# Small matmul tiles for the first two batches' packing attention, and the converted w_out kept in its raw tile

## The chip, the cores and the metric

One core of a Trainium2 chip runs the whole kernel. The metric is the device time of one execution in microseconds (us). A profile is one further execution, taken by the hardware profiler; its span runs from the first to the last recorded instruction.

## The reference

Eight batches of eight heads attend twice: 32 learned "pack" queries p attend to the 576 keys and values of a head, and then the 576 queries q attend to the 32 packed results. Two mixture layers follow on the 4608 x 512 result. The weights of all layers arrive as float32 in the listing below and as float64 words in the kernel.

```python
def sm_attn(qq, kk, vv):
    s = scale * np.matmul(qq, kk.transpose(0, 1, 3, 2))
    s = s - np.max(s, axis=-1, keepdims=True)
    a = np.exp(s)
    a = a / (np.sum(a, axis=-1, keepdims=True) + 1e-09)
    return np.matmul(a, vv)
p_packed = sm_attn(p, k, v)            # pp: 32 x 64 for each head
x = sm_attn(q, p_packed, p_packed)     # 576 x 64 for each head
# x is reshaped to (4608, 512)
h = x @ w_in                           # 512 -> 2048
g = np.maximum(h, 0.0) + alpha * np.minimum(h, 0.0)
x = g @ w_out                          # 2048 -> 512
g = x @ w_gate                         # 512 -> 1536
silu = g * (1.0 / (1.0 + np.exp(-g)))
return silu * (x @ w_val) @ w_out2     # 1536 -> 512
```

## The kernel before

**Folding.** The result of the second attention is never formed. Since it is a2 · pp, with a2 the second softmax, the kernel multiplies pp by w_in once for each batch (ppw, `L811`) and then computes h = a2 · ppw (`L316` to `L318`, three matmuls of high and low parts for one product: a2l x high, a2h x high, a2h x low). g (`L1060`) is split into hi (`L1068`, ScalarE) and lo (`L1070`, GpSimd), and acc = g · w_out is again three matmuls (`L1083`, `L1084`, `L1089`).

**Groups.** A batch has two groups of four heads. The first two batches (groups 0 and 1, then 2 and 3) go through the functions shown at the end of this section, step by step: kT by transposes (`L390`), scores s10 and s11 of p against the two halves of the keys (`logits`, `L417`), their maximum (`L430`, VectorE), E = exp (`L438`, ScalarE), transposes of E, pp (`s_pp`, `L481`), its transpose ppT (`s_ppt`), scores s20 and s21 of q against pp (`logits` again, with the queries read with a stride), the second softmax on VectorE (`L513` to `L550`) and its split into a2h (`L551`) and a2l (`L552`). Later batches use other functions, of which two rows serve below as prices: `L580`, scores by head on 64 x 32 tiles of the array into two banks of PSUM, and `L710`, pp by head on 96 x 32 tiles.

**Weights.** w_in and w_out are fetched by 16 loads (`fetch`, one DMA queue, in order) into raw tiles of float64 words. `widen` makes float32 of them in the raw tile and a second tile `val`: an absolute value on ScalarE (`L234`), five VectorE steps (`L236` to `L267`; `L263` and `L265` replace the last one for four pieces), and a sum on GpSimd (`L277`) that leaves the number in `val`. For w_in, `val` is the weight's own tile; for w_out it is a scratch (`cvd`, and after its two halves are used always `cvb`). `round_piece` then scales it by the signs of alpha (`L301`), rounds it to the high part (`L304`, both ScalarE), and subtracts for the low part (`L305`, GpSimd). The pieces come in a fixed order, here called i0, i2, ... for w_in and o0, o2, ... for w_out: i2 i0 o0 i4 i6 o2 o4 o6 i10 i8 i14 i12 o8 o10 o12 o14. The raw tiles are cva0, cva1, cvc0 and cvc1.

**Order.** The order in which each engine takes its instructions is worked out when the kernel is built: the code issues work word by word from a script ("c" converts a piece, "r" rounds one, "1" does both), and a list scheduler with a timing model of its own reorders it on all engines, for about the first 37 steps of h and acc (the first 215 us). From there on the order of TensorE is written out. Instructions on one engine run in that order and wait there.

Of the kernel before, what the change touches and what calls it, by code (L numbers as in the profile page):

```python
# [11 lines left out]
AF = mybir.ActivationFunctionType  # L12
ALU = mybir.AluOpType
# [4 lines left out]
P = 128  # L18
# [46 lines left out]
BY_POOL = {0, 2, 5, 11}  # L65
# [36 lines left out]
def f32(ap):  # L102
    return ap.bitcast(F32)
# [3 lines left out]
def tile_kernel(  # L107
# [23 lines left out]
    nc = tc.nc  # L131
    B, H, S, D = q.shape
# [6 lines left out]
    HQ = 4  # L139
    M6 = 6  # L140
    PB = S // M6
    NB32 = S // 32
    HS = S // 2
# [57 lines left out]
    def like(ap, other):  # L201

        if len(other.shape) == 2:
            return ap
        return ap.rearrange("p (c f) -> p c f", c=other.shape[1])

    raws, vals, borrowed, queue, marks, spots = [], [], [], [], {}, {}
    fetched, loaded, unsplit = [], [], []
    begun, made, rounded = {}, {}, {}

    def halves_of(ap):

        n = ap.shape[1]
        if len(ap.shape) == 2 and n == 512:
            return [ap]
        return [ap[:, i * n // 2 : (i + 1) * n // 2] for i in range(2)]

    def load():

        src, parts, f = queue.pop(0)  # L220
        raw = raws.pop(0)
        fetch(like(raw, src), src)
        loaded.append((raw, parts, f))
# [3 lines left out]
        with tc.issue_after(fetched[-1].ins) if fetched else ExitStack():  # L227
            fetched.append(nc.sync.dma_start(out=out, in_=in_))

    def widen(raw, val, by_pool=False):  # L230

        words = raw.rearrange("p (n t) -> p n t", t=2)
        low, high = (like(words[:, :, i], val) for i in range(2))
        nc.scalar.activation(out=f32(val), in_=f32(high), func=AF.Abs)  # L234
        yield "v"
        nc.vector.tensor_scalar(  # L236
            out=f32(val), in0=f32(val), scalar1=E_TOP, scalar2=E_LOW, op0=ALU.min, op1=ALU.max
        )
        yield "v"
        nc.vector.tensor_scalar(  # L240
            out=val,
            in0=val,
            scalar1=3,
            scalar2=0x3FFFFFF8,
            op0=ALU.logical_shift_left,
            op1=ALU.bitwise_and,
        )
        yield "v"
        nc.vector.scalar_tensor_tensor(
            out=val,  # L250
            in0=high,
            scalar=0xC0000000,
            in1=val,
            op0=ALU.bitwise_and,
            op1=ALU.bitwise_or,
        )
        yield "v"
        nc.vector.tensor_scalar(
            out=high, in0=val, scalar1=0xFF800000, scalar2=None, op0=ALU.bitwise_and
        )  # L260
        yield "v"
        if by_pool:
            nc.scalar.activation(out=f32(low), in_=low, func=AF.Copy, scale=2.0**-52)  # L263
            for a, b in zip(halves_of(f32(low)), halves_of(f32(high))):
                nc.gpsimd.tensor_tensor(out=a, in0=a, in1=b, op=ALU.mult)  # L265
        else:
            nc.vector.scalar_tensor_tensor(  # L267
                out=f32(low),
                in0=low,
                scalar=2.0**-52,  # L270
                in1=f32(high),
                op0=ALU.mult,
                op1=ALU.mult,
            )
        yield "p"
        for a, b in zip(halves_of(f32(val)), halves_of(f32(low))):
            nc.gpsimd.tensor_tensor(out=a, in0=a, in1=b, op=ALU.add)  # L277

    def convert():

        raw, parts, f = loaded.pop(0)
        dst = parts()
        spots["piece"] = spots.get("piece", -1) + 1
        if f is None:
            val = dst[0].bitcast(U32)
        else:
            val = vals.pop(0) if len(vals) > 1 else vals[0]
        for _ in widen(raw, val, spots["piece"] in BY_POOL):
            pass
        if queue and (spots["piece"] < 4 or not any(raw is t for t in borrowed)):  # L290
            raws.append(raw)
            load()
        unsplit.append((dst, val, f))

    def round_piece():

        dst, val, f = unsplit.pop(0)
        for i in range(2 if f is not None else 0):
            hi, lo = (t[:, i, :] for t in dst)
            full = like(f32(val), dst[0])[:, i, :]  # L300
            nc.scalar.activation(  # L301
                out=full, in_=full, func=AF.Copy, scale=sg[:, f + i : f + i + 1]
            )
            nc.scalar.activation(out=hi, in_=full, func=AF.Copy)  # L304
            nc.gpsimd.tensor_tensor(out=lo, in0=full, in1=f32(hi), op=ALU.subtract)  # L305

    def scratch(name):
        return wpool.tile([P, 2048], U32, tag="D", name=name, bufs=WBUFS["D"])
# [4 lines left out]
    def mm3(o, wts, xs, start, stop, **kw):  # L313
        whi, wlo = wts
        xhi, xlo = xs
        nc.tensor.matmul(o, wlo, xhi, start=start, stop=False, **kw)  # L316
        nc.tensor.matmul(o, whi, xhi, start=False, stop=False, **kw)  # L317
        return nc.tensor.matmul(o, whi, xlo, start=False, stop=stop, **kw)  # L318

    ident = sm.tile([P, P], F32, name="ident")  # L320
    make_identity(nc, ident)
# [9 lines left out]
    def quad(g, ptags=("at",), evac=nc.scalar):  # L331
# [78 lines left out]
        def logits(lhs, rhs, half, name, turned=False):  # L410
            t = pst([P, 512], f"{name}{half}")
            for pr in range(2):
                x = rhs[pr][:, half * HS : (half + 1) * HS]
                if turned:
                    x = rhs[pr].rearrange("q (m p) -> q p m", m=M6)
                    x = x[:, half * PB // 2 : (half + 1) * PB // 2, :]
                nc.tensor.matmul(  # L417
                    t[64 * pr : 64 * pr + 64, :HS],
                    lhs[:, 64 * pr : 64 * pr + 64],
                    x,  # L420
                    start=True,
                    stop=True,
                )
            return t

        def s_s1():
# [48 lines left out]
        def s_pp():  # L475
            pp = pst([P, 512], "pp")
            for m in range(M6):
                for pr in range(2):
                    e = st["ET"][m // 4]
                    c = (m % 4) * P + 64 * pr  # L480
                    nc.tensor.matmul(  # L481
                        pp[64 * pr : 64 * pr + 64, :P].rearrange("p (h d) -> p h d", h=2),
                        e[:PB, c : c + 64],
                        st["v"][:, 2 * pr : 2 * pr + 2, m, :],
                        start=(m == 0),
                        stop=(m == M6 - 1),
                    )
            pb = ppbd[g % 2]
            for h in range(HQ):
                r = slice(32 * h, 32 * h + 32)  # L490
                c = slice((h % 2) * D, (h % 2) * D + D)
                marks[f"pp{g}"] = nc.scalar.activation(
                    out=pb[r, c], in_=pp[r, c], func=AF.Copy, scale=st["rs"][r, 3:4]
                )

        def s_ppt():
# [292 lines left out]
    def pp_win(b, j):  # L789

        t = wtile("C", F32R, f"ppw{b}_{j}")
        ppw[b, j] = t
        (w,) = win[j]
        if b > 1:
            o = [
                ps.tile([P, 512], F32, tag="at", name=f"ppw{b}_{j}{r}", bufs=2) for r in range(2)
            ]
            heads8(o, ppT[b, None], [w[:, i, :] for i in range(H // 2)])
            for r in range(2):
                nc.scalar.activation(out=t[:, r, :], in_=o[r], func=AF.Copy)  # L800
            for r in range(2):
                nc.vector.tensor_tensor(
                    out=t[:, NQ + r, :], in0=o[r], in1=f32(t[:, r, :]), op=ALU.subtract
                )
            return
        for q2 in range(NQ):
            o = ps.tile([P, 512], F32, tag="at", name=f"ppw{b}_{j}{q2}", bufs=2)
            with behind():
                for pr in range(2):
                    r = slice(64 * pr, 64 * pr + 64)  # L810
                    last = nc.tensor.matmul(  # L811
                        o[r, :], ppT[b, q2][:, r], w[:, 2 * q2 + pr, :], start=True, stop=True
                    )
            done(last)
            nc.scalar.activation(out=t[:, q2, :], in_=o, func=AF.Copy)
            nc.vector.tensor_tensor(
                out=t[:, NQ + q2, :], in0=o, in1=f32(t[:, q2, :]), op=ALU.subtract
            )
# [27 lines left out]
    def run(script):  # L846
        for word in script.split():
            word, _, held = word.partition(":")
            with ExitStack() as behind_marks:
                for name in held.split(",") if held else ():  # L850
                    behind_marks.enter_context(tc.issue_after(marks[name].ins))
                for w in ("c", "r") if word == "1" else (word,):
                    do(w)

    def do(word):
        if word in early:
# [558 lines left out]
```

## Time and profile before

| what | us |
|---|---|
| three runs | 1646.09, 1644.81, 1646.09 (median 1646.09) |
| the profiled execution | 1643.74 |
| its span | 1642.0 |
| TensorE busy in it | 1591.0 (97%) |
| VectorE, ScalarE, GpSimd busy | 848.1, 678.0, 717.1 |

The profiled execution took 1.7 us more than its span and 2.35 us less than the median of the runs. TensorE is idle for about 50 us of the span in all.

### The profile page before, as it was taken

To read this page: it belongs to the slowest core of one execution; us is meant where nothing else is said; L and a number is where in the kernel's file an instruction comes from. 1 tells how busy PE (TensorE), PEld (TensorE's weight loads), DVE (VectorE), ACT (ScalarE), POOL (GpSimd) and SP (SyncE) were. 2 spreads that over 40 slices of the span, in tenths; PEclk is the share of its full clock that TensorE was granted. 3 is DMA by queue.
4 is the path that set the end of the run, shared out by engine and by line. 5 is a ranking of instruction groups with operands and counts; after the bars stand their busy time and mean duration, and the time that the engine had idled before them with its cause. 6 is when DMAs were issued, how large, how long until landed. Compare 5 with 4: busy or idle time off the path is not lost.

```text
span 1642.0 us, 28420 instructions
## 1 busy us (share of the span) xinstructions
PE 1591.0 (97%) x10709; PEld 1446.6 (88%) x10709; DVE 848.1 (52%) x1473; ACT 678.0 (41%) x1504; POOL 717.1 (44%) x764
## 2 busy tenths in 40 slices
PE   7599999999999999999999999999999999999997
PEld 4368899989899999999999999999999999999996
DVE  6858757676767676765224433432442443334222
ACT  6575655555555655555312322322232232223212
POOL 4738665666666666664223223222322232322222
PEclk8699999999999999999999999999999999999999
DMA  9405365655545564653644564554465465435442
GB/s 286 147 28 136 111 181 143 158 139 157 153 132 154 137 166 117 171 158 106 243 155 173 180 218 138 196 200 171 158 215 183 150 214 177 180 139 214 149 165 84
DMA packets 224058, 266.11 MB, mean 162 GB/s; under 512 B 128160, under 2 KB 185520, under 8 KB 223920
## 3 DMA queue, kind: packets, MB, share of 16 engines
q1 hardware_dynamic: 223920, 264.30, 50.8%
q8 instruction: 84, 1.38, 0.3%
q14 instruction: 54, 0.44, 0.1%
HBM read 214.70 MB, written 49.55 MB: 161 GB/s over the span
## 4 chain that ended last, share of the span: by engine, by line
issue 38%; PE 37%; POOL 16%; DVE 5%; ACT 2%; DMA 1%; POOLq 0%; ACTq 0%; DVEq 0%
POOL pl L1302 9%; PE acc L1083 7%; PE acc L1084 7%; PE acc L1089 7%; POOL s L1282 4%; PE h L316 4%; PE h L318 4%; PE h L317 3%; PE ppw L580 1%; PE s L580 1%; POOL cva L277 1%; PE s L417 1%; POOL lo L1070 1%; POOL xr L1143 0%; PE pp L710 0%
## 5 line engine op out<-in xcount | busy, mean ns | idle before, releaser
L1070 POOL TENSOR_TENSOR lo<-g,hi 128x288 fp32r<-128x288 f32 x256 | 233.4, 913 | 236.1 <-ACT hi L1068 188.9
L1282 POOL TENSOR_TENSOR s<-s,u 128x384 f32<-128x384 f32 x72 | 73.0, 1015 | 490.1 <-ACT s L1276 490.1
L1060 DVE SCALAR_TENSOR_TENSOR g<-h,sg,m 128x288 f32<-128x288 f32 x256 | 130.5, 511 | 173.5 <-ACT m L1057 142.4
L1239 DVE TENSOR_TENSOR u<-yb,p 128x384 f32<-128x384 f32 x144 | 80.1, 556 | 254.8 <-PE yb L318 254.8
L1302 POOL TENSOR_TENSOR pl<-s,ph 128x384 fp32r<-128x384 f32 x144 | 145.4, 1031 | 106.8 <-ACT ph L1300 106.8
L1239 DVE TENSOR_TENSOR u<-vb,u 128x384 f32<-128x384 f32 x144 | 80.4, 558 | 197.6 <-PE vb L318 197.4
L316 PE MATMUL h<-a2h,ppw 128*128 128x288 f32 x512 | 159.4, 311 | 16.0 <-ACT a2h L551 9.1
L318 PE MATMUL o<-wp,ph 128*128 128x512 f32 x432 | 171.5, 397 | 0.0
L317 PE MATMUL o<-wp,ph 128*128 128x512 f32 x432 | 170.9, 396 | 0.0
L316 PE MATMUL o<-wp,pl 128*128 128x512 f32 x432 | 168.7, 391 | 0.9 <-POOL pl L1302 0.9
L1057 ACT ACTIVATE m<-h,sal 128x288 f32<-128x288 f32 x256 | 126.9, 497 | 101.4 <-PE h L318 100.9
L1276 ACT ACTIVATE s<-p 128x384 f32<-128x384 f32 x72 | 37.9, 526 | 301.7 <-DVE p L1239 301.7
L1068 ACT ACTIVATE hi<-g 128x288 fp32r<-128x288 f32 x256 | 113.0, 442 | 111.4 <-DVE g L1060 108.7
L318 PE MATMUL h<-a2l,ppw 128*128 128x288 f32 x512 | 152.2, 298 | 2.2 <-POOL a2l L552 2.2
L317 PE MATMUL h<-a2h,ppw 128*128 128x288 f32 x512 | 152.1, 297 | 0.0
L316 PE MATMUL yb<-ring,gv 128*128 128x384 f32 x432 | 145.9, 338 | 0.3 <-DVE u L1239 0.3
L317 PE MATMUL yb<-ring,gv 128*128 128x384 f32 x432 | 144.4, 334 | 0.0
L318 PE MATMUL yb<-ring,gv 128*128 128x384 f32 x432 | 144.4, 334 | 0.0
L316 PEld LDWEIGHTS h<-a2h,ppw 128*128 128x128 f32 x512 | 97.5, 191 | 45.3 <-issue 12.9
L1300 ACT ACTIVATE ph<-s 128x384 fp32r<-128x384 f32 x144 | 69.8, 519 | 121.6 <-DVE s L1280 121.6
L318 PEld LDWEIGHTS h<-a2l,ppw 128*128 128x128 f32 x512 | 97.1, 190 | 4.6 <-POOL a2l L552 3.8
L317 PEld LDWEIGHTS h<-a2h,ppw 128*128 128x128 f32 x512 | 97.8, 191 | 0.0
(245 smaller groups left out, 4129.9 us busy)
## 6 DMA issues: line engine op xcount, KB each, us to landing
gv<-wgvd SPq DMA_DIRECT2D x144, 896.0 KB, 6.2
wgvd<-cva SPq DMA_DIRECT2D x84, 256.0 KB, 3.0
v<-in_v_dram SPq DMA_DIRECT2D x16, 576.0 KB, 5.9
out_dram<-os SPq DMA_DIRECT2D x12, 768.0 KB, 3.9
cva<-in_moe_w_in_dram SPq DMA_DIRECT2D x7, 1024.0 KB, 7.2
kr<-in_k_dram SPq DMA_DIRECT2D x96, 72.0 KB, 2.8
qr<-in_q_dram SPq DMA_DIRECT2D x96, 72.0 KB, 2.8
x1d<-x1s SPq DMA_DIRECT2D x24, 288.0 KB, 3.5
```

The costliest lines, as they stand in the source:

```text
L316: nc.tensor.matmul(o, wlo, xhi, start=start, stop=False, **kw)
L317: nc.tensor.matmul(o, whi, xhi, start=False, stop=False, **kw)
L318: return nc.tensor.matmul(o, whi, xlo, start=False, stop=stop, **kw)
L1057: begun[it] = marks[f"u{it}"] = nc.scalar.activation(out=m, in_=hp, func=AF.Copy, scale=sal[:, f : f + 1])
L1060: made[it] = marks[f"m{it}"] = nc.vector.scalar_tensor_tensor(out=g32, in0=hp, scalar=sg[:, f : f + 1], in1=m, op0=ALU.mult, op1=ALU.max)
L1070: nc.gpsimd.tensor_tensor(out=lo, in0=x, in1=f32(hi), op=ALU.subtract)
L1083: nc.tensor.matmul(acc[dc], lo[:, f % WP, c], ghi, start=start, stop=False)
L1084: last = nc.tensor.matmul(acc[dc], hi[:, f % WP, c], ghi, start=False, stop=False)
L1089: last = nc.tensor.matmul(acc[dc], hi[:, f % WP, c], glo, start=False, stop=stop)
L1239: return nc.vector.tensor_tensor(out=out, in0=bank, in1=x, op=ALU.add)
L1282: latest.append(nc.gpsimd.tensor_tensor(out=s2, in0=s2, in1=u3, op=ALU.mult))
L1302: nc.gpsimd.tensor_tensor(out=lo, in0=x, in1=f32(hi), op=ALU.subtract)
```

## The change

Three edits. **Scores and ppw**: each pair of heads was one matmul of 128 rows x 64 columns of the array, with a stationary operand in which half of the entries are zeros; now each head has a matmul of its own on 64 rows x 32 columns, so four matmuls stand where two stood, all four into one bank of PSUM, on different partitions. **pp**: a pair of heads was one matmul of 96 x 64 over 128 columns of v, half of the result unused; now each head is one of 96 x 32 over its own 64 columns. **Conversion**: for w_out, the sum is written into the odd words of the raw tile, and scaling and rounding work there. So the scratch is free after the sum, and the raw tile is free (and its next load issued) only after the rounding.

```diff
     def convert():
...
-        for _ in widen(raw, val, spots["piece"] in BY_POOL):
+        full = None
+        if f is not None:
+            full = f32(raw).rearrange("p (n t) -> p n t", t=2)[:, :, 1]
+        for _ in widen(raw, val, spots["piece"] in BY_POOL, full):
             pass
-        if queue and (spots["piece"] < 4 or not any(raw is t for t in borrowed)):
-            raws.append(raw)
-            load()
-        unsplit.append((dst, val, f))
+        unsplit.append((dst, full, f, raw, spots["piece"]))
+        if f is None:
+            round_piece()
 
     def round_piece():
...
+        if queue and (n < 4 or not any(raw is t for t in borrowed)):
+            raws.append(raw)
+            load()
...
+    def tiles_of(pr):
+
+        for r in range(2):
+            n = 64 * pr + 32 * r
+            yield slice(64 * r, 64 * r + 64), slice(n, n + 32)
...
-                nc.tensor.matmul(
-                    t[64 * pr : 64 * pr + 64, :HS],
-                    lhs[:, 64 * pr : 64 * pr + 64],
-                    x,
-                    start=True,
-                    stop=True,
-                )
+                for rows, n in tiles_of(pr):
+                    nc.tensor.matmul(t[n, :HS], lhs[rows, n], x[rows], start=True, stop=True)
...
-                for pr in range(2):
-                    e = st["ET"][m // 4]
-                    c = (m % 4) * P + 64 * pr
+                for h in range(HQ):
+                    c = (m % 4) * P + 32 * h
                     nc.tensor.matmul(
-                        pp[64 * pr : 64 * pr + 64, :P].rearrange("p (h d) -> p h d", h=2),
-                        e[:PB, c : c + 64],
-                        st["v"][:, 2 * pr : 2 * pr + 2, m, :],
+                        pp[32 * h : 32 * h + 32, :D],
+                        st["ET"][m // 4][:PB, c : c + 32],
+                        st["v"][:, h, m, :],
...
                 for pr in range(2):
-                    r = slice(64 * pr, 64 * pr + 64)
-                    last = nc.tensor.matmul(
-                        o[r, :], ppT[b, q2][:, r], w[:, 2 * q2 + pr, :], start=True, stop=True
-                    )
+                    for rows, n in tiles_of(pr):
+                        last = nc.tensor.matmul(
+                            o[n, :],
+                            ppT[b, q2][rows, n],
+                            w[rows, 2 * q2 + pr, :],
+                            start=True,
+                            stop=True,
+                        )
```

The scheduler orders the first 215 us anew. Three places show it. The line numbers of the changed kernel are higher: its L438, L446 and L454 are L430, L438 and L446 of before, its L520 is L513, its L278, L304 and L308 are L277, L301 and L305, its L559 is L552, its L1082 is L1070.

VectorE, around the maximum of group 2's first scores (`mx_2`), in the kernel before; `a_1` is group 1's second softmax, `s2t_0` group 0's, `cvb0` the scratch of w_out's pieces:

```order
L550 STREAM_TRANSPOSE a_1_418<-s2t_1_393 128x288
L430 TENSOR_REDUCE mx_2_643<-s10_2_637 128x1
L430 TENSOR_REDUCE mx_2_643<-s11_2_640 128x1
L433 TENSOR_REDUCE mx_2_643<-mx_2_643 128x1
L434 TENSOR_SCALAR mx_2_643<-mx_2_643 128x1
L446 TENSOR_SCALAR sums_2_649<-sums_2_649 128x1
L513 STREAM_TRANSPOSE s2t_0_380<-s21_0_669 128x288
```

The same place on VectorE in the changed kernel:

```order
L557 STREAM_TRANSPOSE a_1_454<-s2t_1_427 128x288
L236 TENSOR_SCALAR cvb0_106<-cvb0_106 128x1024
L240 TENSOR_SCALAR cvb0_106<-cvb0_106 128x1024
L249 SCALAR_TENSOR_TENSOR cvb0_106<-cvc1_104,cvb0_106 128x1024
L438 TENSOR_REDUCE mx_2_689<-s10_2_679 128x1
L258 TENSOR_SCALAR cvc1_104<-cvb0_106 128x1024
L438 TENSOR_REDUCE mx_2_689<-s11_2_684 128x1
L267 SCALAR_TENSOR_TENSOR cvc1_104<-cvc1_104 128x1024
L441 TENSOR_REDUCE mx_2_689<-mx_2_689 128x1
L442 TENSOR_SCALAR mx_2_689<-mx_2_689 128x1
L454 TENSOR_SCALAR sums_2_695<-sums_2_695 128x1
L520 STREAM_TRANSPOSE s2t_0_412<-s21_0_715 128x288
```

The five steps of piece o6's conversion, which stood behind `s2t_0`, have moved up around group 2's maximum.

ScalarE, ahead of that place, in the kernel before; `hi3` and `m_3` belong to the fourth step of h, `a2h_1` to group 1, `wo1h` is w_out's second tile:

```order
L1057 ACTIVATE m_3_662<-h3_654,sal_99 128x288
L349 ACTIVATE kT1_2_617<-kt10_2_618 64x3x96 x2
L304 ACTIVATE wo1h_601<-cvb0_106 128x512
L301 ACTIVATE cvb0_106<-cvb0_106,sg_98 128x512
L349 ACTIVATE kT1_2_617<-kt11_2_624 64x3x96 x2
L1068 ACTIVATE hi3_665<-g32_3_661 128x288
L551 ACTIVATE a2h_1_416<-a_1_418 128x288
```

And in the changed kernel:

```order
L1069 ACTIVATE m_3_708<-h3_700,sal_99 128x288
L362 ACTIVATE kT1_2_657<-kt10_2_658 64x3x96
L307 ACTIVATE wo1h_641<-cvc0_103 128x512
L362 ACTIVATE kT1_2_657<-kt10_2_658 64x3x96
L304 ACTIVATE cvc0_103<-cvc0_103,sg_98 128x512
L234 ACTIVATE cvb0_106<-cvc1_104 128x1024
L1080 ACTIVATE hi3_711<-g32_3_707 128x288
L362 ACTIVATE kT1_2_657<-kt11_2_664 64x3x96 x2
L558 ACTIVATE a2h_1_452<-a_1_454 128x288
```

Piece o6's first step (`L234`) now stands ahead of `hi3` and of the second half of kT1; the rounding of o4 works in `cvc0`, its raw tile.

GpSimd, about 130 us into the kernel before, around a2l of groups 2 and 3 (`s2t_3` is group 3's softmax, `wi2` a tile of w_in):

```order
L536 TENSOR_TENSOR s2t_3_1096<-s2t_3_1096,sx_3_1097 128x576
L1070 TENSOR_TENSOR lo13_1231<-g32_13_1225,hi13_1229 128x288
L1070 TENSOR_TENSOR lo14_1268<-g32_14_1262,hi14_1266 128x288
L277 TENSOR_TENSOR wi2_1015<-wi2_1015,cva1_102 128x2x256 x2
L552 TENSOR_TENSOR a2l_3_1213<-a_3_1214,a2h_3_1212 128x576
L552 TENSOR_TENSOR a2l_2_1250<-a_2_1251,a2h_2_1249 128x576
L1070 TENSOR_TENSOR lo15_1295<-g32_15_1289,hi15_1293 128x288
```

And in the changed kernel:

```order
L1082 TENSOR_TENSOR lo12_1261<-g32_12_1255,hi12_1259 128x288
L559 TENSOR_TENSOR a2l_3_1305<-a_3_1306,a2h_3_1304 128x576
L559 TENSOR_TENSOR a2l_2_1342<-a_2_1343,a2h_2_1341 128x576
L1082 TENSOR_TENSOR lo13_1323<-g32_13_1317,hi13_1321 128x288
L1082 TENSOR_TENSOR lo14_1360<-g32_14_1354,hi14_1358 128x288
L278 TENSOR_TENSOR wi2_1095<-wi2_1095,cva1_102 128x2x256 x2
```

The two a2l stand ahead of two lo and of the sums of `wi2`, and the softmax's multiplication in front of them is no longer on this engine.

## Rows read from the trace of the kernel before

**Rows 1.** Busy time in stretches: window, length, engines, TensorE's granted clock, DMA.

```profile
0.00:63.50 63.50, 34.61 (x164) 20.71 (x164) 50.01 (x81) 33.69 (x69) 38.14 (x47) 0.78 0.87 246
63.50:104.00 40.50, 36.47 (x251) 27.53 (x251) 22.73 (x45) 30.74 (x75) 21.08 (x19) 0.93 0.16 54
104.00:130.00 26.00, 25.69 (x155) 18.34 (x156) 22.23 (x38) 15.87 (x35) 11.06 (x10) 1.00 0.30 81
130.00:215.00 85.00, 78.75 (x559) 69.09 (x558) 61.39 (x83) 49.77 (x104) 66.25 (x56) 0.98 0.41 118
...
141.00:144.00 3.00, 3.00 (x14) 2.66 (x13) 2.41 (x6) 2.26 (x4) 3.00 (x3) 0.51 0.86 134
```

**Rows 2.** TensorE's waits from 44 to 70 us: total, times, longest.

```profile
PE h L316 <- DVE g L1060: 5.3, 1, 5.3
```

**Rows 3.** TensorE's timeline: start, duration, instruction, tile, matmuls grouped.

```profile
87.30 1.53 PE L481 MATMUL pp<-v,ET 96*64 96x128 f32 x24
...
97.55 0.71 PE L417 MATMUL s<-kT,pT 128*64 128x288 f32 x4
...
104.89 1.23 PE L417 MATMUL s<-qT,ppT 128*64 128x288 f32 x4
...
123.07 1.94 PE L811 MATMUL ppw<-wi,ppT 128*64 128x512 f32 x8
...
220.51 0.88 PE L710 MATMUL pp<-v,ET 96*32 96x64 f32 x48
...
238.41 0.71 PE L580 MATMUL s<-qT,ppT_2b 64*32 64x288 f32 x16
```

**Rows 4.** Piece o4's load: the page's part 6, then timelines of SyncE, GpSimd, ScalarE.

```profile
cva<-in_moe_w_in_dram SPq DMA_DIRECT2D x7, 1024.0 KB, 7.2
...
36.88 0.38 SPq L228 DMA_DIRECT2D cvc<-in_moe_w_out_dram  x1
...
44.27 1.47 POOL L305 TENSOR_TENSOR wo0l<-cvd,wo0h 128x512 fp32r<-128x512 f32 x1
...
56.94 1.14 ACT L234 ACTIVATE cvb<-cvc 128x1024 f32<-128x1024 f32 x1
```

**Rows 5.** VectorE's and ScalarE's timelines from 35 to 87 us.

```profile
36.89 0.69 DVE L236 TENSOR_SCALAR cvd<-cvd 128x1024 f32<-128x1024 f32 x1 [1.02 <-ACT cvd L234]
...
76.73 0.94 DVE L430 TENSOR_REDUCE mx<-s 128x1 f32<-128x288 f32 x2 [1.98 <-PE s L417]
...
86.63 1.22 DVE L267 SCALAR_TENSOR_TENSOR cvc<-cvc 128x1024 f32<-128x1024 uint32 x1
...
78.08 0.50 ACT L438 ACTIVATE E<-s,mx 128x288 f32<-128x288 f32 x1 [0.52 <-DVE mx L434]
...
79.77 1.14 ACT L234 ACTIVATE cvb<-cvc 128x1024 f32<-128x1024 f32 x1
```

**Rows 6.** TensorE's timeline: idle time before an instruction and its releaser, in brackets.

```profile
75.99 1.18 PE L417 MATMUL s<-kT,pT 128*64 128x288 f32 x6 [0.49 <-ACT kT L349]
...
82.85 0.47 PE L390 MATMUL kt<-ident,k 96*128 96x96 f32 x3 [1.05 <-DVE ppw L816]
...
96.17 0.40 PE L1083 MATMUL acc<-hi,wo1l 128*128 128x288 f32 x1 [0.77 <-POOL wo1l L305]
...
99.88 0.53 PE L463 MATMUL et<-ident,E 128*96 128x128 f32 x3 [0.90 <-ACT E L438]
```

**Rows 7.** TensorE's waits from 100 to 216 us.

```profile
PE h L318 <- POOL a2l L552: 2.0, 1, 2.0
PE ppw L811 <- DVE ppw L816: 1.6, 1, 1.6
```

**Rows 8.** GpSimd's timeline at 133 us, ScalarE's at 182 us.

```profile
133.16 3.02 POOL L277 TENSOR_TENSOR wi<-wi,cva 128x512 f32<-128x512 f32 x2
136.14 4.20 POOL L552 TENSOR_TENSOR a2l<-a,a2h 128x576 fp32r<-128x576 f32 x2
...
182.37 1.14 ACT L234 ACTIVATE cvb<-cva 128x1024 f32<-128x1024 f32 x1 [0.33 <-POOL wo2l L305]
```

More of the change, by code (lines that the diff above doesn't have):

```diff
@@ L228, in fetch, with widen @@
             fetched.append(nc.sync.dma_start(out=out, in_=in_))
-    def widen(raw, val, by_pool=False):
+    def widen(raw, val, by_pool=False, into=None):
         words = raw.rearrange("p (n t) -> p n t", t=2)
@@ L275, in widen @@
         yield "p"
-        for a, b in zip(halves_of(f32(val)), halves_of(f32(low))):
-            nc.gpsimd.tensor_tensor(out=a, in0=a, in1=b, op=ALU.add)
+        into = f32(val) if into is None else like(into, val)
+        for o, a, b in zip(*(halves_of(t) for t in (into, f32(val), f32(low)))):
+            nc.gpsimd.tensor_tensor(out=o, in0=a, in1=b, op=ALU.add)
     def convert():
@@ L287, in convert @@
             val = vals.pop(0) if len(vals) > 1 else vals[0]
-        for _ in widen(raw, val, spots["piece"] in BY_POOL):
-            pass
-        if queue and (spots["piece"] < 4 or not any(raw is t for t in borrowed)):
-            raws.append(raw)
-            load()
-        unsplit.append((dst, val, f))
+        full = None
+        if f is not None:
+            full = f32(raw).rearrange("p (n t) -> p n t", t=2)[:, :, 1]
+        for _ in widen(raw, val, spots["piece"] in BY_POOL, full):
+            pass
+        unsplit.append((dst, full, f, raw, spots["piece"]))
+        if f is None:
+            round_piece()
     def round_piece():
-        dst, val, f = unsplit.pop(0)
+        dst, sums, f, raw, n = unsplit.pop(0)
         for i in range(2 if f is not None else 0):
             hi, lo = (t[:, i, :] for t in dst)
-            full = like(f32(val), dst[0])[:, i, :]
+            full = like(sums, dst[0])[:, i, :]
             nc.scalar.activation(
@@ L492, in s_pp @@
                 marks[f"pp{g}"] = nc.scalar.activation(
-                    out=pb[r, c], in_=pp[r, c], func=AF.Copy, scale=st["rs"][r, 3:4]
+                    out=pb[r, c], in_=pp[r, :D], func=AF.Copy, scale=st["rs"][r, 3:4]
                 )
@@ L851, in run @@
                     behind_marks.enter_context(tc.issue_after(marks[name].ins))
-                for w in ("c", "r") if word == "1" else (word,):
-                    do(w)
+                do("c" if word == "1" else word)
+                if word == "1" and unsplit:
+                    do("r")
     def do(word):
```

## The prediction

> **What bounds the kernel now.** I read the busy shares first, then busy time by stretch, then TensorE's waits in the stretches that the change touches, then single instructions. TensorE is busy for 97% of the span (the table), so only two things can move the time: shorter TensorE work, and shorter waits of TensorE. The change touches the two batches of the first 215 us; behind them TensorE's order is written out and no instruction differs. The stretches tell them apart [rows 1]: up to 63.5 us TensorE works 34.6 us of 63.5 while VectorE works 50.0, and TensorE's last wait there is 5.3 us for VectorE's g [rows 2]. So the start-up belongs to VectorE, and a faster matmul there buys nothing. From 63.5 to 104 TensorE idles 40.5 - 36.5 = 4.0 us, from 104 to 130 0.3 us, from 130 to 215 6.25 us. That is 10.6 us in all, the most that better order could give there, and the ground that worse order can lose.
>
> **The tiles.** Scores first: a pair of matmuls on 128 x 64 tiles takes 0.71 us with contiguous keys, and eight 64 x 32 tiles of a later batch also take 0.71 [rows 3]. So the two column tiles of a pair already run side by side, and tiles of half the size save no time: the stream of 288 columns is what lasts, whatever the tile. With the strided queries a pair takes 1.23 us [rows 3], again the length of one stream. ppw, four 512-column matmuls in 1.94 us, is the same case. I cost all three at +0.02 us a call for the added instructions, +0.3 in sum for the 24 calls or so; bounds are nothing, and, if tiles can't share a bank, the third rival's price.
>
> pp does shrink, since its moving operand falls from 128 to 64 columns: 1.53 us before, 0.88 us for the same shape in a later batch [rows 3], so 0.65 us a group. Groups 0 and 1 lie in VectorE's start-up and give nothing; groups 2 and 3 give **-1.3 us**. Bounds: nothing, if E is what TensorE waits for there, and -2.6.
>
> The reordering costs something too. In the new TensorE order group 2's s20 has its two pairs apart, with other matmuls between, so that one strided stream's 1.2 us is paid twice and half of the overlap of rows 3 goes: +1.1. One ppw call is split the same way (0.97 us for half of the 1.94): +0.45 after rounding down for what overlaps. Together **+1.85 us** with the 0.3 above; bounds 0 and +2.5.
>
> **The conversion: its start.** In the start-up VectorE has the same steps as before. Only one of its idle times can be filled, 1.02 us ahead of `L236`, where it waits for ScalarE [rows 5], since group 1's work now stands ahead. I take **-0.8 us**, bounds 0 and -2.5 (the order of some twenty VectorE steps changes there). The raw tile is now held until it is rounded. Worst placed is o4's load, issued at 36.88; o0's rounding ends with a subtraction at 45.7, so the load moves by up to 9 us. A load of this size lands in 7.2 us, thus at 53, and o4's first step runs at 56.94 [rows 4]: hidden with 4 us to spare, while the loads of q and v behind it on the one DMA queue move too; they are group 3's, whose pp comes behind the one at 87.30 [rows 3]. If it were not hidden, each us late would be a us of VectorE's chain.
>
> **The conversion: the stretch from 70 to 87 us.** With the scratch free earlier, the scheduler puts o6's five VectorE steps ahead of and between group 2's maximum. They are three of 0.69 us and two of 1.22 [rows 5], 4.5 us; VectorE had 1.98 us of idle there [rows 5], so the maximum, and ScalarE's E of 78.08, come 2.5 us later. TensorE's s21 of group 0 needs a bank that E frees and stands right behind: a new stall of 2.5. ScalarE's `L234` of 1.14 us [rows 5] now stands ahead of hi3, on which acc waits: 1.1 in place of the 0.49 for kT [rows 6]. And ppw's first copy now stands behind o6's scaling on ScalarE, so the wait for ppw is 1.3 in place of 1.05 [rows 6]. Sum 4.9 - 1.54 = **+3.4 us**; bounds 0 (if TensorE arrives late enough for other reasons) and +5. Some comes back at once: w_out's second tile is finished earlier, so its wait of 0.77 goes, and of the 0.90 for group 3's E a late TensorE sees perhaps 0.2 [rows 6]: **-1.5 us**.
>
> **The conversion: 130 to 215 us.** Three of the waits there hang on the conversion's order. The longest is 1.99 us for a2l: GpSimd does two sums of 3.02 us first and a2l only from 136.14 [rows 7, 8]. The new order has a2l ahead of them. In the 3 us from 141 TensorE then ran at a granted clock of 0.51 [rows 1], its lower level of 1.2 GHz, which cost another 1.5. The waits for ppw hang on the conversions on VectorE, and those start late because `L234` waits for the scratch until the rounding's last subtraction [rows 7, 8]; the raw tile takes that wait off. Against it: GpSimd is busy 66 of these 85 us and VectorE 61 [rows 1], and a TensorE that arrives sooner meets them sooner. I take 2.5 of the 6.25 as left, and half of the clock's 1.5 as saved: **-4.4 us**; bounds 0 and -7.7.
>
> **The sum.** -0.8 + 3.4 - 1.5 - 1.3 + 1.85 - 4.4 = -2.75 us against 1643.74 of the profiled execution: 1641.0. The median of the runs lies 2.35 above that execution, so on its level 1646.09 - 2.75 = 1643.3, and I say 1643.4. A difference under 0.2% (3.3 us) can't be told from no change here, and this sum lies just inside.
>
> **Rivals.** *The freed scratch pays in full.* The new stalls at 75 to 83 us don't come, because all of VectorE's start-up moves forward: -2.5 there in place of -0.8, +1.0 in place of +3.4, and -5 in the last stretch: -2.5 + 1.0 - 1.5 - 1.3 + 1.85 - 5 = -7.5, or 1638.6. For it speaks that VectorE carries the start-up; against it that the order shows E's maximum behind the conversion. Chance 0.25.
>
> *The new place of o6 is not made up.* The stall of 2.5 us at s21 is longer than the 1.99 after which the clock fell for 3 us, so TensorE falls to the lower level again, +1.5; and later VectorE and GpSimd, busy 22 of 26 us and 66 of 85 [rows 1], keep TensorE at their own pace, so that of the -4.4 only -1 comes: -0.8 + 3.4 + 1.5 - 1.5 - 1.3 + 1.85 - 1 = +2.15, and +5 with both upper bounds of the two stall terms. That ends near 1649.5, slower than before; it decides from the point where less than 1 us of the last stretch's idle time goes. Against it: what a2l waits for is moved ahead of it whatever VectorE does. Chance 0.18, of which 0.14 slower.
>
> *Two row tiles can't write one bank at a time.* Then the four matmuls run as two after two, and each call takes twice its length: from 65 us on four calls of 0.71, six of 1.23 and fourteen of 0.97 [rows 3], 23.8 us, or 1667. The trace shows column tiles sharing a bank without loss, and row tiles only in two banks (`L580`). The tiles here lie on different partitions of the bank, for which nothing in the trace speaks of a conflict. Chance 0.07. The Trainium skill, page "TensorEngine Tiling (Array Packing)", section "Restrictions and Gotchas", says that different row tiles can't access one PSUM bank simultaneously; the page "PSUM — Partial Sum Buffer" says in its table that different quadrants of a bank may be accessed at the same time. By the first the result would be this rival's, by the second the sum above; no run here shows either yet.
>
> **How the numbers follow.** The likeliest case has 0.50, its own range 1639 to 1647, with 0.17 faster by over 0.2% and 0.33 within it. Faster: 0.17 + 0.25 = 0.42; slower: 0.14 + 0.07 = 0.21; within: 0.33 + 0.04 = 0.37. The range of 1636.5 to 1651 reaches past the first rival by 2 us and past the second by 1.5, and leaves out the third and the tails of the others.
>
> **What would show it.** Right: pp groups of 0.88 us; score and ppw calls as long as before; TensorE's s21 of group 0 waiting for E by about 2.5 us near 80; the kt of 82.85 [rows 6] some 2.4 us later; no wait for a2l near 140 and a clock of 1.00 behind it; the steps behind 215 us as long as before. Wrong: calls of doubled length (the third rival); a low clock near 82; o4's first step waiting for its load; or waits for ppw from 180 to 195 that are as long as before.

## The result, and the profile after

The changed kernel is slower: 1660.64 us (median of four runs, 1658.12 to 1661.21) against 1646.09, a ratio of 1.0087 with a 95% interval of 1.0069 to 1.0104. That is 14.5 us, outside the range of the prediction and on the other side of its likeliest case. The profiled execution took 1661.21 us, its span is 1659.4. It is the slowest of its kernel's executions and the one of before the fastest of its own, so the spans differ by 17.4 us where the medians differ by 14.5.

Part 1 of the page answers to the table of busy times before. TensorE's busy time grew by 2 us only, so 15 of these 17.4 us are idle time:

```profile
PE 1593.1 (96%) x10933; PEld 1442.7 (87%) x10933; DVE 852.7 (51%) x1473; ACT 681.5 (41%) x1504; POOL 722.3 (44%) x764
```

Busy time by stretch (columns as in [rows 1]), cut at the places in the work where rows 1 cut: the first g, group 3's pp. The last three rows are stretches of low clock.

```profile
0.00:65.60 65.60, 31.57 (x244) 18.33 (x244) 51.42 (x81) 34.21 (x69) 37.44 (x47) 0.71 0.84 239
65.60:113.80 48.20, 37.62 (x336) 27.32 (x336) 25.91 (x45) 32.12 (x78) 22.82 (x19) 0.89 0.14 46
...
86.00:90.00 4.00, 3.75 (x24) 0.91 (x24) 1.69 (x6) 3.96 (x11) 2.57 (x3) 0.57 0.02 4
109.00:114.00 5.00, 4.78 (x68) 3.90 (x68) 0.03 (x1) 4.32 (x11) 0.00 (x0) 0.66 0.00 0
198.00:210.00 12.00, 9.49 (x43) 3.39 (x44) 8.52 (x12) 6.94 (x14) 6.80 (x7) 0.57 0.40 127
```

The start-up is 2.1 us longer; the stretch to group 3's pp took 48.2 us where before took 40.5. From 70 us on TensorE fell to its lower clock of 1.2 GHz three times: behind the wait of 86 us, near 110 us behind a wait of 1.66 us for E, and from 199 us on behind a wait for g. Of what was busy in the three rows, 43, 34 and 43% is the clock's: 1.6 + 1.6 + 4.1 = 7.3 us, where before lost 1.5 [rows 1].

TensorE's timeline, the rows that answer to [rows 3] and [rows 6]:

```profile
86.25 0.70 PE L431 MATMUL s<-qT,ppT 64*32 64x288 f32 x4 [4.35 <-ACT E L446]
98.66 0.88 PE L488 MATMUL pp<-v,ET 96*32 96x64 f32 x48
132.59 1.92 PE L818 MATMUL ppw<-wi,ppT 64*32 64x512 f32 x16
199.25 0.61 PE L323 MATMUL h<-a2h,ppw 128*128 128x288 f32 x1 [2.23 <-DVE g L1072]
```

The matmuls do what was forecast: pp 0.88 us for 1.53, ppw 1.92 for 1.94. The two waits are what is new. What E waited for stands on VectorE, between group 1's transpose and the maximum; o6's five steps are L236, L240, L249, L258 and L267:

```profile
78.47 0.69 DVE L236 TENSOR_SCALAR cvb<-cvb 128x1024 f32<-128x1024 f32 x1 [1.55 <-ACT cvb L234]
79.20 1.18 DVE L240 TENSOR_SCALAR cvb<-cvb 128x1024 uint32<-128x1024 uint32 x1
80.42 1.70 DVE L249 SCALAR_TENSOR_TENSOR cvb<-cvc,cvb 128x1024 uint32<-128x1024 uint32 x1
82.04 0.45 DVE L438 TENSOR_REDUCE mx<-s 128x1 f32<-128x288 f32 x1
82.41 1.41 DVE L258 TENSOR_SCALAR cvc<-cvb 128x1024 uint32<-128x1024 uint32 x1
83.73 0.45 DVE L438 TENSOR_REDUCE mx<-s 128x1 f32<-128x288 f32 x1
84.10 1.21 DVE L267 SCALAR_TENSOR_TENSOR cvc<-cvc 128x1024 f32<-128x1024 uint32 x1
...
85.60 0.50 ACT L446 ACTIVATE E<-s,mx 128x288 f32<-128x288 f32 x1 [4.12 <-DVE mx L442]
...
78.78 1.06 POOL L1082 TENSOR_TENSOR lo<-g,hi 128x288 fp32r<-128x288 f32 x1 [1.07 <-ACT hi L1080]
80.09 0.94 POOL L559 TENSOR_TENSOR a2l<-a,a2h 128x288 fp32r<-128x288 f32 x1 [0.26 <-ACT a2h L558]
81.00 2.27 POOL L308 TENSOR_TENSOR wo1l<-cvc,wo1h 128x512 fp32r<-128x512 f32 x1
```

VectorE first stands idle for 1.55 us until ScalarE has made o6's absolute value, and then the five steps last 6.2 us, not the 4.5 that I had added up from rows in which GpSimd was idle: while GpSimd works from 78.8 to 83.3 us, steps of 0.69 and 1.22 us last 1.18 to 1.70. E starts at 85.60 us, 7.5 us later than before [rows 5].

### The profile page after: what moved, and what is told of

The parts are those of the page before. It is cut to its first block, busy times and chain, and to the rows that moved or that the text cites. A ratio compares the mean times of both kernels' runs of the same rounds, so it can differ in the third digit from the quotient of the medians.

```text
span 1659.4 us, 28858 instructions
## 1 busy us (share of the span) xinstructions
PE 1593.1 (96%) x10933; PEld 1442.7 (87%) x10933; DVE 852.7 (51%) x1473; ACT 681.5 (41%) x1504; POOL 722.3 (44%) x764
## 4 chain that ended last, share of the span: by engine, by line
PE 38%; issue 38%; POOL 15%; DVE 4%; DMA 3%; ACT 2%; SPq 1%; POOLq 0%; ACTq 0%; DVEq 0%
POOL pl L1314 9%; PE acc L1095 7%; PE acc L1101 7%; PE acc L1096 7%; POOL s L1294 4%; PE h L323 4%; PE h L324 3%; PE h L325 3%; PE ppw L587 1%; DMA cvc<-in_moe_w_out_dram 1%; PE s L587 1%; POOL cva L278 1%; PE ppw L818 1%; PE s L431 1%; POOL xr L1155 0%
## 5 line engine op out<-in xcount | busy, mean ns | idle before, releaser
L1082 POOL TENSOR_TENSOR lo<-g,hi 128x288 fp32r<-128x288 f32 x256 | 234.3, 917 | 234.6 <-ACT hi L1080 188.8
```

The costliest lines, as they stand in the source:

```text
L1082: nc.gpsimd.tensor_tensor(out=lo, in0=x, in1=f32(hi), op=ALU.subtract)
```

## The experiments

**How the order was held.** In most of these kernels the order of every engine in the first part is written out, instruction by instruction, as it stood in another kernel, by an order edge from each instruction to the one before it; where a pair by heads stands for one matmul, both stand in its place. The edges carry no semaphore (`NoSync`). The traces bear the order out: up to 215 us the four kernels in the old order (the first three below and pp_old_order) have the instructions of before in the same sequence on TensorE, VectorE, ScalarE and GpSimd. That writing it out costs nothing by itself is seen at conv_old_order below, which takes as long as before.

```diff
+def pin(nc, tc):
+    by = {i.name: i for i in nc.cur_bb.bb.instructions}
+    why = m.DependencyInfo(m.DependencyClass.NoSync, m.DependencyReason.DATA)
+    for names in PINNED.values():
...
+        for first, then in zip(names, names[1:]):
+            tc.add_manual_dep(by[then], first, why, reason="pinned")
...
     with _tile.TileContext(nc, schedule_with_timeline_sim=True) as tc:
         tile_kernel(tc, *args)
+        pin(nc, tc)
```

**The edits against the order.** Four kernels: the tile edits alone, the conversion edit alone, and all three, each in the order of the kernel before; and the conversion edit with the old tiles in the order of the changed kernel. The theories: the new order costs (1), the small tiles cost through the clock (2), the raw tile held until its rounding costs (3).

tiles_old_order: 

> Only the tile edits (scores, ppw, pp by head), conversion as before, and every engine's order in the first part written out as it stood in the kernel before (where two matmuls stood, the four or the pair by head stand). Theory 1, the new order is what costs: 1643 to 1646 us, by pp's 1.3 us at most faster than before, and score and ppw calls as long as before. Theory 2, tiles that use half of the array's rows cost of themselves, because TensorE then runs longer at its lower clock after a wait: 1650 or more, with stretches at a granted clock near 0.5 where before has 1.00. Theory 3, the conversion costs: as theory 1.

conv_old_order: 

> Only the conversion edit (sum into the raw tile, raw tile held until rounded), tiles as before, every engine's order in the first part as in the kernel before. Theory 1, order: 1642 to 1647 us. Theory 2, tiles: the same. Theory 3, the raw tile held until its rounding makes loads and so the conversions behind them late: 1650 or more, with a ScalarE first step (the absolute value) that waits for its load.

all_old_order: 

> All three edits, every engine's order in the first part as in the kernel before. Theory 1, order: 1641 to 1647 us, so the whole loss of 14.5 us is gone. Theories 2 or 3: 1655 or more; a mixture would lie between.

old_tiles_new_order: 

> The conversion edit with the tiles of before, every engine's order in the first part as in the changed kernel. Theory 1, order: 1656 to 1662 us, with the wait for E near 86 us of 4 us or more. Theory 2, tiles: 1648 to 1653, since the clock then recovers during the ppw calls near 88 and 200 us (8.3 us for four calls in the changed kernel, at a granted clock of 0.50). Theory 3 alone: as theory 1.

| kernel | median us | ratio to before, 95% interval |
|---|---|---|
| tiles_old_order | 1647.79 | 1.0012 (1.0003 to 1.0020) |
| conv_old_order | 1645.35 | 1.0001 (0.9992 to 1.0010) |
| all_old_order | 1647.05 | 1.0003 (0.9995 to 1.0012) |
| old_tiles_new_order | 1656.77 | 1.0057 (1.0044 to 1.0071) |

All three edits in the old order cost nothing that can be told from no change; the new order with the old tiles costs 10.8 us of the 14.5. Theory 1 holds for these 10.8, though its sign in old_tiles_new_order came in part only: TensorE waits 1.85 us for E there, not 4, and 2.13 for ScalarE's kT ahead of that. Theory 3 falls by conv_old_order's time: ScalarE's first steps wait for their loads 4.5 us in sum from 20 to 216 us, where before has 2.9, and it costs nothing. Theory 2 can hold at most for the rest. The tile edits came out 2 us above theory 1's range, by their interval 0.5 to 3.3 us slower than before.

**Which edit turns the order.** One edit alone, the order left to the scheduler.

conv_free_order: 

> The conversion edit alone, tiles as before, the order left to the scheduler. If the conversion edit is what makes the scheduler move o6 ahead of E: 1652 to 1660 us. If it takes the tile edits to turn the order: 1643 to 1648.

tiles_free_order: 

> The tile edits alone, conversion as before, the order left to the scheduler. If only the conversion edit turns the order for the worse: 1645 to 1649. If any edit that changes the scheduler's picture of the first part costs about as much: 1652 or more.

Measured: 1657.26 us (1.0063, 1.0047 to 1.0079) and 1651.94 us (1.0037, 1.0024 to 1.0049). Either edit alone is enough to turn the order for the worse, and in both o6's first steps stand ahead of E (the tiles' time lies 0.06 us under its theory's range). With the tiles alone, o6's first VectorE step comes between the maximum of the halves and that of both, though its scratch isn't free yet; so the freed scratch, by which the prediction explained the move, isn't needed for it. VectorE waits in front of the step:

```profile
82.01 0.69 DVE L236 TENSOR_SCALAR cvb<-cvb 128x1024 f32<-128x1024 f32 x1 [1.78 <-ACT cvb L234]
82.62 0.15 DVE L434 TENSOR_REDUCE mx<-mx 128x1 f32<-128x2 f32 x1
```

**Where in the order the loss lies.** The changed kernel in three mixed orders: only o6 moved back behind E; the old order up to group 3's pp and the new one behind it; and the reverse.

o6_moved_back: 

> The changed kernel with its order written out, except that piece o6's conversion and rounding stand behind group 2's E again, near where the kernel before has them, on VectorE, ScalarE and GpSimd. If the early conversion of o6 is what makes E late and starts the loss (the wait of 4.35 us for E at 86 us, and the lag of 2.1 us at 73 us that is 8.8 at 86): the wait for E is under 1 us and the time is 1648 to 1655. If the loss comes from all over the new order: 1657 or more.

old_then_new: 

> All three edits, the order written out: every engine in the order of the kernel before up to group 3's pp (103.9 us there), and behind it in the order of the changed kernel. If the loss is made ahead of that place (the early o6 and the start-up) and only carried on: 1646 to 1650 us. If the new order also loses behind it (the low clock near 200 us, the waits for g): 1651 to 1656.

new_then_old: 

> All three edits, the order of the changed kernel up to group 3's pp (113.8 us there), and behind it the order of the kernel before. If the loss is made ahead of that place: 1655 to 1661 us. If half of it comes behind: 1651 to 1655. The sum of this loss and that of the opposite splice should be near the whole, 13.6 us over all edits in the old order.

Measured: 1655.78 us (1.0060, 1.0048 to 1.0073), 1649.81 us (1.0032, 1.0020 to 1.0044) and 1654.64 us (1.0054, 1.0041 to 1.0067). By the ranges the first lies between both theories, old_then_new (two of its six runs at 1652.92 and 1654.68) says that the loss is made ahead, and new_then_old that half of it comes behind; so the medians alone don't settle where. How much later than in the profiled execution of before the n-th g (from 0) starts on VectorE, in us, shows where each loses (its own start there in the first row):

| kernel | 0 | 4 | 13 | 24 | 45 | 255 |
|---|---|---|---|---|---|---|
| before, start | 63 | 86 | 128 | 163 | 223 | 795 |
| changed | 2.1 | 8.8 | 10.5 | 9.4 | 13.7 | 15.2 |
| old_tiles_new_order | 1.0 | 8.1 | 12.3 | 10.8 | 13.5 | 14.2 |
| all_old_order | 1.3 | 1.5 | 1.2 | 1.7 | 1.9 | 0.8 |
| o6_moved_back | 2.8 | 5.7 | 8.1 | 7.1 | 9.9 | 9.3 |
| old_then_new | 1.8 | 1.9 | 3.5 | 2.0 | 6.3 | 5.2 |
| new_then_old | 3.0 | 9.6 | 9.4 | 9.3 | 9.5 | 8.4 |
| a2l_first | 1.0 | 1.1 | 1.0 | 5.6 | 6.3 | 7.0 |

The last row's kernel (below) is the kernel before up to 130 us, and yet 1.0 late at the first g: about 1 us there differs from one execution to the next. Against all_old_order the early part of the new order costs 7.6 us (1654.64 - 1647.05), the late part 2.8 (1649.81 - 1647.05), together 10.4 of 13.6. The missing 3.2 us are no more than the intervals of these four kernels leave open (1.4 to 2.9 us to either side of each). At the 46th g the early part costs 9.5 - 1.9 = 7.6 us, the late one 6.3 - 1.9 = 4.4 and the whole order 13.7 - 1.9 = 11.8, so there the two parts add up. The early loss is made between the first g and the fifth, around group 2's E. With o6 moved back, TensorE waits there for 0.83 us in place of 4.35, but the same stretch has another wait, for g:

```profile
82.43 0.69 PE L431 MATMUL s<-qT,ppT 64*32 64x288 f32 x4 [0.83 <-ACT E L446]
92.52 0.47 PE L403 MATMUL kt<-ident,k 96*128 96x96 f32 x3 [2.64 <-DVE g L1072]
```

So o6's place is worth 4.9 us of the 14.5 (1660.64 - 1655.78), less than the first reading asked for. The late loss goes with a low clock. Stretches of old_then_new, and the same ones of new_then_old behind them:

```profile
190.00:198.00 8.00, 5.38 (x22) 2.05 (x22) 4.95 (x8) 6.60 (x12) 5.82 (x6) 0.58 0.65 213
198.00:204.00 6.00, 5.49 (x32) 2.75 (x33) 3.96 (x6) 2.28 (x4) 2.56 (x2) 0.70 0.00 0
```

```profile
190.00:198.00 8.00, 7.25 (x53) 6.66 (x52) 6.51 (x11) 5.08 (x11) 4.50 (x6) 1.00 0.37 131
198.00:204.00 6.00, 4.34 (x37) 1.39 (x37) 4.64 (x7) 5.20 (x10) 4.15 (x4) 1.00 0.58 197
```

At 0.58 and 0.70 the first loses 5.38 x 0.42 + 5.49 x 0.30 = 3.9 us, behind a wait of 2.23 us for g; the old order has no such stretch there, though before lost 1.5 at 141 us. All five kernels that hold the changed kernel's late order have this wait, 2.22 or 2.23 us long. In the changed kernel ScalarE's step m for that g stands behind the scaling of a w_out piece, which waits for GpSimd's sum; this is read from the trace, and no run moves it:

```profile
197.42 0.77 ACT L304 ACTIVATE cva<-cva,sg 128x512 f32<-128x512 f32 x1 [0.44 <-POOL cva L278]
198.09 0.48 ACT L1069 ACTIVATE m<-h,sal 128x288 f32<-128x288 f32 x1
```

**Is it the array's rows?** The tiles of the changed kernel work on half as many rows in sum as the pair did.

```diff
-            yield slice(64 * r, 64 * r + 64), slice(n, n + 32)
+            yield slice(0, P), slice(n, n + 32)
```

full_rows_new_order: 

> The changed kernel with its order written out, but each small score and ppw tile takes all 128 rows (the zeros of the stationary operand too) and 32 columns: as many matmuls in the same places, and twice the rows at work. If the share of the array at work decides how long TensorE stays at its lower clock after a wait, the four ppw calls near 201 us (8.3 us at 0.50 in the changed kernel) and the two near 88 us speed up, and the time is that of the old tiles in this order, 1655 to 1658. If it does not, 1659 to 1662 as the changed kernel.

Measured: 1661.63 us (1.0094, 1.0081 to 1.0106), as the changed kernel, and two ppw calls at 204 us last 3.14 us where 1.92 is their time at the full clock; the stretch behind their start has a granted clock of 0.50:

```profile
204.23 3.14 PE L818 MATMUL ppw<-wi,ppT 128*32 128x512 f32 x16
```

```profile
204.00:206.00 2.00, 2.00 (x14) 0.46 (x16) 1.47 (x3) 2.00 (x5) 1.06 (x3) 0.50 0.85 266
```

The low clock comes with all rows at work too, and the time is no better. The old tiles in this order have it as well. Of the four ppw calls near 201 us each two took 3.63 and 3.43 us in the changed kernel and 3.27 and 1.94 with the old tiles, so at this place theory 2's sign came; but TensorE then waited 2.35 us for ppw's copy on VectorE where the changed kernel waits 1.26, and from 75 to 215 us both have the same granted clock (first the changed kernel, then old_tiles_new_order):

```profile
75.00:215.00 140.00, 123.32 (x928) 93.81 (x927) 94.35 (x142) 86.66 (x184) 90.61 (x73) 0.94 0.30 85
75.00:215.00 140.00, 124.56 (x783) 96.96 (x784) 93.32 (x138) 84.99 (x181) 88.66 (x70) 0.94 0.28 82
```

At the 46th g the two kernels are as late (13.7 and 13.5 us), so theory 2 doesn't account for the loss.

**Two terms of the sum by themselves.** The wait for a2l taken away in the kernel before, and pp by head alone in the old order.

```diff
+L552 TENSOR_TENSOR a2l_3, a2l_2
 L277 TENSOR_TENSOR wi2 x2
-L552 TENSOR_TENSOR a2l_3, a2l_2
```

a2l_first: 

> The kernel before, its order written out, with one move: GpSimd's two a2l of groups 2 and 3 ahead of the two sums of wi2. If the 1.99 us that TensorE waits at 140 us and the 1.5 us of the lower clock behind it are lost for good: 1642 to 1644 us. If VectorE and GpSimd set the pace there anyway and the wait only comes back later: 1645 to 1647.

pp_old_order: 

> Only pp by head, order of the kernel before. If TensorE's own work is what the 40 us before 104 us are made of: 1.3 us faster than before, 1644.7. If TensorE waits there for other engines whatever it does, the waits grow by what pp saves: no change, 1645.5 to 1646.5, and waits of TensorE from 80 to 104 us that are 1 us or so longer in sum.

a2l_first measured 1651.11 us (1.0032, 1.0019 to 1.0045): neither theory, 5 us slower. The sums of wi2 that stood in front were needed first, by ppw:

```profile
140.53 1.12 PE L811 MATMUL ppw<-wi,ppT 128*64 128x512 f32 x2 [5.07 <-POOL wi L277]
```

pp_old_order measured 1648.01 us (1.0011, 1.0002 to 1.0020): no gain, rather a loss of 0.3 to 3.3 us; in its profile 1.2 of the 1.5 us by which the last g is late lie ahead of the first g. The pp call lasts 0.88 us, and two waits behind it grow by 0.4 and 0.6 us; they were 0.77 [rows 6] and 0.87 us:

```profile
97.50 0.40 PE L1082 MATMUL acc<-hi,wo1l 128*128 128x288 f32 x1 [1.15 <-POOL wo1l L305]
...
212.38 0.40 PE L1082 MATMUL acc<-hi,wo3l 128*128 128x288 f32 x1 [1.51 <-POOL wo3l L305]
```

What the pp edit costs at the start is seen at o0's load. ScalarE's first step of o0, in the kernel before and in pp_old_order:

```profile
25.37 1.18 ACT L234 ACTIVATE cvd<-cvc 128x1024 f32<-128x1024 f32 x1
27.19 1.15 ACT L234 ACTIVATE cvd<-cvc 128x1024 f32<-128x1024 f32 x1 [2.89 <-DMA cvc<-in_moe_w_out_dram]
```

In the traces of all nine kernels with pp by head this load lands 3.8 to 4.0 us behind the load of q in front of it, in the five others 2.4 to 2.5. In the nine a transfer of 16 KB on the DMA queue that the page calls instruction falls into it, at 24.9 to 26.3 us; in the five that transfer comes at 28.3 to 32.3 us, when o0 has landed. That the one delays the other is read from these times, and no run moves it.

No run was clearly faster than the kernel before.

## Why the prediction was wrong

**The tiles' lengths: right.** Scores and ppw take as long as before, pp 0.88 us, and in the new order the strided scores that stand apart take 1.15 us each, as forecast. So the third rival is out: four tiles on two row groups write one bank side by side, the sixteen matmul records of two ppw calls in 1.92 us, as the eight of before in 1.94 [rows 3]. The Trainium skill's page "TensorEngine Tiling (Array Packing)", section "Restrictions and Gotchas", says that different row tiles can't access one PSUM bank simultaneously; the runs of this case, in which the row tiles write different partitions, don't bear that out in time. The sentence that the prediction sets against it, from the Trainium skill's page "PSUM — Partial Sum Buffer" (its table under "Terms"), stands there beside accesses by different engines; it was no forecast for row tiles.

**What they are worth: wrong.** The step "only two things can move the time: shorter TensorE work, and shorter waits" took each 0.65 us of pp for a gain. Up to 215 us TensorE is released by VectorE, ScalarE and GpSimd so often that its savings become waits (pp_old_order, tiles_old_order): nothing in place of -1.3. That added instructions could cost through the loads stood in no term.

**The start-up: wrong, and in part open.** -0.8 was forecast, +2.1 came. About 1 us of it goes with the tile edits, by o0's load: old_tiles_new_order is 1.0 late at the first g, as a2l_first is with no change there. In the old order the conversion edit makes no difference (0.4). o4's load stayed hidden, as forecast.

**70 to 87 us: the mechanism right, the size half.** o6 ahead of E, the stall at s21, hi3 behind ScalarE's first step: all came. The term +3.4 measured 8.8 - 2.1 = 6.7. Mis-sized was "E come 2.5 us later": the five steps last 6.2 us beside a busy GpSimd and not 4.5, VectorE stood idle for 1.55 in front of them, and E came 5.4 us late beyond the start-up; the stall was 4.35. The clock then fell (0.57 over 4 us), which I had put into a rival with a chance of 0.18 and not into the sum. Of the -1.5 that should come back, the wait for w_out's second tile did go, but group 3's E was waited for 1.66 us and not 0.2.

**130 to 215 us: wrong, the step that failed most.** I took 2.5 of 6.25 us of waits as left, since the order showed the waits' causes moved away (with half of the clock's 1.5 that makes -4.5, not -4.4). They were moved: a2l is waited for no more, and the clock at 141 us is 1.00. Only the softmax's multiplication is still on GpSimd (L543 at 131.7 us), against what stands under "The change". But the new order has other waits in their place, first of all four for g (TensorE's waits from 104 to 230 us, columns as in [rows 7]; the one for E lies at 108 us, ahead of this stretch):

```profile
PE h L323 <- DVE g L1072: 4.3, 4, 2.2
PE et L471 <- ACT E L446: 1.7, 1, 1.7
```

Forecast -4.4, measured 13.7 - 10.5 = +3.2 from the 14th g to the 46th. These are the stretches, of before and of the changed kernel:

```profile
127.70:223.10 95.40, 89.15 (x679) 79.23 (x678) 68.61 (x100) 55.92 (x117) 70.05 (x59) 0.98 0.44 124
138.20:236.80 98.60, 91.79 (x704) 77.82 (x702) 65.89 (x96) 55.13 (x114) 68.14 (x57) 0.95 0.40 115
```

TensorE idles 6.8 us where it idled 6.25, so nothing of the idle time was won, and the low clock at 198 to 210 us costs 4.1 where the one at 141 us cost 1.5. That a freed scratch is worth nothing by itself shows conv_old_order (1.0001), and that a wait's removal must be followed to the next one shows a2l_first.

**The rivals.** The second had the way it went, o6's new place not made up and the clock falling, and was priced at +2 to +5 where 14.5 came: it took the old order's waits as the most that could be lost. The larger part of what moved the time was no edit but the scheduler's new order.

**What is left, and what stays open.** The changed kernel and old_tiles_new_order differ by 3.9 us in their medians, by 4.2 in their profiled executions and by 0.2 us at the 46th g. That difference arises behind 215 us, where both have the same instructions, and 2.8 us of it in two waits of TensorE near 1108 and 1526 us (1.34 and 1.42), which old_tiles_new_order hasn't. In front of each, VectorE's copy of results waits for the last store to land, first in the changed kernel, then in the other:

```profile
1106.94 0.69 DVE L1338 COPY os<-o 128x512 f32<-128x512 f32 x1 [4.71 <-DMA out_dram<-os]
1104.47 0.69 DVE L1340 COPY os<-o 128x512 f32<-128x512 f32 x1 [3.31 <-DMA out_dram<-os]
```

All nine kernels with tile edits have these two waits, 1.6 to 3.0 us in sum, and in all nine a 16 KB transfer of the instruction queue comes some 3 us ahead of each of these two copies; in the five others none comes within 10 us of either. From 150 to 720 us behind the last g every second copy waits over 2 us for a store, 70 copies in all fourteen profiles: the 21 with such a transfer 2.2 to 3.2 us ahead wait 3.6 to 5.0 us, the 49 others 3.1 to 3.4. So this rest goes with the tile edits' added instructions and not with the order; that the transfer delays the store is read from these times, and no run moves it. Why the new order's late part makes TensorE wait for g is read from one trace only. What brings a low clock on and what ends it isn't known: behind the wait for a2l, 1.99 us in before and 2.02 in all_old_order, it fell in the first and stayed at 1.00 in the second.

## What to carry to other kernels

Where a scheduler orders the program, an edit has two prices: that of its instructions and that of the order that it sets off. Writing the old order out with the new instructions, and the new order with the old ones, tells them apart in two runs; here the first was nothing that could be told and the second 10.8 of 14.5 us. And a wait seen in a trace isn't there to be won until the next thing that the engine needs has been dated: moving a2l ahead by 3 us of GpSimd's work bought a wait of 5.07 us for that work.

## What the runs showed of the hardware that was not expected

VectorE's conversion steps of 128 x 1024 last 0.69 and 1.22 us while GpSimd is idle, and often longer while it works, up to 1.78 and 2.30 in the kernel before; an estimate from the lone rows was short by 1.7 us in five steps. Low clock after a wait lasted from about 3 us (before, behind 1.99 us) to about 10 us (changed, behind 2.23 us), through 8.5 us of matmuls. With 190 to 440 more instructions recorded, a 16 KB transfer of the instruction queue came at 25 to 26 us in place of 28 or later, within the load of o0, and that load landed 1.2 to 1.6 us later behind the one in front of it.
